# Pooled attention and a gated MLP on one core: keys tiled by head pair, leftovers in 32-column matmul tiles, keys turned by DMA

## Chip, cores and metric

One core of one Trainium2 chip. The metric is the device time of one execution in microseconds (us), the median of the runs. The kernel before took 309.03 us (308.74 to 309.35, 4 runs, the profiled one among them). The granted TensorE clock (the share of full speed that the throttle let through), averaged over the execution, is 0.997 to 1.000 in the kernel before.

Names: PE is TensorE, PEld its weight loads, DVE VectorE, ACT ScalarE, POOL GpSimd, SP SyncE, which issues most DMAs.

## The reference

```python
batch, n_heads, seq, head_dim = (8, 8, 576, 64)       # q, k, v; d_model 512, d_ff 2048
k_p = k.reshape(B, H, 72, 8, D).mean(axis=3)           # keys and values pooled by 8: 72 rows per head
v_p = v.reshape(B, H, 72, 8, D).mean(axis=3)
attn = softmax(q @ k_p.transpose / sqrt(D))            # per head: 576 x 72
x = (attn @ v_p).transpose(0, 2, 1, 3).reshape(B * S, H * D)   # 4608 tokens x 512
h = x @ w_in
return (h - np.tanh(h)) @ w_out                        # 4608 x 512, float32
```

## The kernel before

The MLP runs over nine groups of 512 tokens (0 to 8), each with an h phase (64 matmuls for `x @ w_in`, tanh and subtraction) and an o phase (64 matmuls for `@ w_out`). The attention of batch `nb` is woven into the o phase of group `nb - 1`, in rounds `u` of four o matmuls. Batch 0 is done alone at the start, and batch 1 lies in group 0's o phase.

A batch has 8 heads x 72 = 576 pooled key rows. Before, they lie in five tiles of 128 rows (the last half full) without regard to heads; a head pair's 144 rows cross tile borders, so three of the five score tiles need two accumulating matmuls:

```python
PAIRS = [[0], [0, 1], [1, 2], [2, 3], [3]]             # head pairs that a tile of keys touches
for n, hp in enumerate(PAIRS[t]):
    nc.tensor.matmul(dst, lhsT=KB[b % 2][:, hp * KBW + t * 128 : hp * KBW + (t + 1) * 128],
                     rhs=qTs[b][:, hp, c0:c1], start=(n == 0), stop=(n == len(PAIRS[t]) - 1))
```

KB holds the pooled keys, turned (head dimension on partitions) and padded with zeros. Before, PE turns the keys of batches 1 to 7 in the first round of the o phase, and DVE and ACT copy them to KB. The loads of the start:

```python
load_rows(k_rows, k_raw[0], 0, 0, 2)                   # SP: 512 KB of keys
load_q0(0, 4)                                          # ACT's queue: 512 KB of q
load_rows(k_rows, k_raw[0], 0, 4, 5)                   # SP: the 64 leftover rows, 128 KB
load_rows(k_rows, k_raw[0], 0, 2, 4)                   # SP: the other 512 KB of keys
load_q0(4, 8)                                          # ACT's queue: 512 KB of q
nc.scalar.dma_start(out=t0[:QT, :, R, :], in_=...)     # ACT's queue: the tail of q, 128 KB
# ... cut; later, batch 0's own order of work:
k_turn(0, 2); q_pe_transpose(0, (0, 1), "act")
pool_k(0, nc.vector, 4, 5); pool_k(0, nc.vector, 2, 4)
scores_wide(0, (0, 1)); warm_pe(5)                     # warm_pe: matmuls on zeros, to keep PE busy
k_turn(2, 5); q_pe_transpose(0, (2, 3), "act")
v_pe_pool(0, 3); scores_wide(0, (2,)); v_pe_pool(3, 5); scores_wide(0, (3, 4))
```

Batch 1's transposes of x, one round after the product that they turn:

```python
if u >= 9:
    if pend is not None:
        x_pe_transpose(1, *pend)
        pend = None
    if u <= 13:
        pend = (u - 9, av(1, u - 9, ps_any, False))
```

The softmax here doesn't subtract the row's maximum and nothing guards it: scores larger than these inputs give would overflow.

Of the kernel before, what the change touches and what calls it, by code (L numbers as in the profile page):

```python
# [27 lines left out]
NT = 5  # L28
D1 = D + 1
SCALE = 1.0 / (POOL * float(D) ** 0.5)  # L30
# [3 lines left out]
def kernel(  # L34
# [28 lines left out]
    v_rows = v.rearrange("b h (g j) d -> b (h g) (j d)", j=POOL)  # L63

# [4 lines left out]
    mask = const.tile([128, NT, 3, 1], FP32, name="mask")  # L69
    k_raw = [const.tile([128, NT, POOL * D], FP32, name=f"k_raw{i}") for i in range(2)]  # L70
    v_raw = [const.tile([128, NT, POOL * D], FP32, name=f"v_raw{i}") for i in range(2)]
    KBW = NT * 128
    STEP = KBW + 2 * G
    KB = [const.tile([128, NHP * KBW + 2 * G + KBW], BF16, name=f"KB{i}") for i in range(2)]
    q_bf = const.tile([128, R + 1, H, D], BF16, name="q_bf")
    warm = const.tile([128, 1], FP32, name="warm")
    VB = [const.tile([128, NT, 3, D1], BF16, name=f"VB{i}") for i in range(2)]
# [18 lines left out]
    def load_rows(src, dst, b, t0, t1):  # L96
        if t1 <= 4:
            return nc.sync.dma_start(
                out=dst[:, t0:t1, :],
                in_=src[b, t0 * 128 : t1 * 128, :].rearrange("(t p) n -> p t n", p=128),  # L100
            )
        return nc.sync.dma_start(out=dst[0:64, 4, :], in_=src[b, 512:576, :])

    def load_k(b, cuts=(0, 4, 5)):
        return [load_rows(k_rows, k_raw[b % 2], b, a, z) for a, z in zip(cuts, cuts[1:])]

    def load_v(b, cuts=(0, 4, 5)):
        return [load_rows(v_rows, v_raw[b % 2], b, a, z) for a, z in zip(cuts, cuts[1:])]
# [84 lines left out]
    def pool_v(b, eng, t0=0, t1=NT):  # L193
        r = v_raw[b % 2].rearrange("p t (j d) -> p t j d", d=D)[:, t0:t1, :, :]
        n = t1 - t0
        eng.tensor_tensor(  # L196
            out=r[:, :, 0:4, :], in0=r[:, :, 0:4, :], in1=r[:, :, 4:8, :], op=ALU.add
        )
        eng.tensor_tensor(  # L199
            out=r[:, :, 0:2, :], in0=r[:, :, 0:2, :], in1=r[:, :, 2:4, :], op=ALU.add  # L200
        )
        eng.tensor_tensor(
            out=r[:, :, 0, :], in0=r[:, :, 0, :], in1=r[:, :, 1, :], op=ALU.add
        )
        return eng.tensor_tensor(  # L205
            out=VB[b % 2][:, t0:t1, :, 0:D],
            in0=r[:, :, 0:1, :].to_broadcast([128, n, 3, D]),
            in1=mask[:, t0:t1, :, :].to_broadcast([128, n, 3, D]),
            op=ALU.mult,
        )  # L210

    def k_transpose(b, alloc):
        kd = kdups.pop(b)
        kb = KB[b % 2]
        for half in range(2):
            ps = alloc([128, 2, 2, G], FP32, "kT_ps")
            flat = ps.rearrange("p i a g -> p (i a g)")
            c = half * 4 * G
            while c < (half + 1) * 4 * G:
                t = c // 128  # L220
                n = min((t + 1) * 128, (half + 1) * 4 * G) - c
                nc.tensor.matmul(  # L222
                    flat[:, c - half * 4 * G : c - half * 4 * G + n],
                    lhsT=kd[:, t, :, :].rearrange("p a d -> p (a d)"),
                    rhs=ident[:, c - t * 128 : c - t * 128 + n],
                    start=True,
                    stop=True,
                )
                c += n
            step = KBW + 2 * G  # L230
            for par, eng in ((0, nc.vector.tensor_copy), (1, nc.scalar.copy)):
                off = 2 * half * step + par * G
                pr = slice(par * D, (par + 1) * D)
                eng(  # L234
                    out=kb[pr, off : off + 2 * step].rearrange("p (i x) -> p i x", x=step)[
                        :, :, 0:G
                    ],
                    in_=ps[pr, :, par, :],
                )

    E_tiles = {}
    PAIRS = [[0], [0, 1], [1, 2], [2, 3], [3]]

    def scores(b, t):
# [3 lines left out]
        qT = qTs[b]  # L248
        hs = S // 2
        for half in range(2):  # L250
            ps = ps_a.tile([128, hs], FP32, name="s_ps", tag="ps_a")
            for n, hp in enumerate(PAIRS[t]):
                nc.tensor.matmul(  # L253
                    ps[:, :],
                    lhsT=KB[b % 2][:, hp * KBW + t * 128 : hp * KBW + (t + 1) * 128],
                    rhs=qT[:, hp, half * hs : (half + 1) * hs],
                    start=(n == 0),
                    stop=(n == len(PAIRS[t]) - 1),
                )
            nc.scalar.activation(  # L260
                out=E[:, t, half * hs : (half + 1) * hs], in_=ps[:, :], func=ACT.Exp, scale=SCALE
            )

    XM = [
        [(0, 1, 3, 0), (1, 0, 3, 1), (2, 0, 1, 3)],
        [(2, 1, 3, 0), (3, 0, 3, 1), (4, 0, 1, 3)],
    ]
# [18 lines left out]
    def score_mms(b, t, dst, c0, c1):  # L286
        for n, hp in enumerate(PAIRS[t]):
            nc.tensor.matmul(  # L288
                dst,
                lhsT=KB[b % 2][:, hp * KBW + t * 128 : hp * KBW + (t + 1) * 128],  # L290
                rhs=qTs[b][:, hp, c0:c1],
                start=(n == 0),
                stop=(n == len(PAIRS[t]) - 1),
            )

    def av_half(b, blk, half, x_sb, alloc):
# [4 lines left out]
        for n, (t, s0, s1, h0) in enumerate(XM[half]):  # L301
            nc.tensor.matmul(  # L302
                ps[:, h0 : h0 + s1 - s0, :].rearrange("p h d -> p (h d)"),
                lhsT=E[:, t, c0 : c0 + 128],
                rhs=vb[:, t, s0:s1, :].rearrange("p h d -> p (h d)"),
# [179 lines left out]
    def load_q0(h0, h1):  # L485
# [5 lines left out]
    load_rows(k_rows, k_raw[0], 0, 0, 2)  # L491
    load_q0(0, 4)
    load_rows(k_rows, k_raw[0], 0, 4, 5)
    load_rows(k_rows, k_raw[0], 0, 2, 4)
# [3 lines left out]
    nc.vector.memset(zeros, 0.0)  # L498
# [3 lines left out]
    nc.vector.memset(k_raw[0][64:128, 4, :], 0.0)  # L502
# [3 lines left out]
    nc.gpsimd.memset(v_bf[64:128, 4, :], 0.0)  # L506
    nc.gpsimd.memset(q_bf[64:128, R, :, :], 0.0)
    nc.gpsimd.memset(mask[:, :, :, :], 1.0)
    mflat = mask.rearrange("p t s o -> p t (s o)")
    nc.gpsimd.affine_select(  # L510
        out=mflat,
        in_=mflat,
        compare_op=ALU.is_ge,
        fill=0.0,
        base=G,
        pattern=[[-16, NT], [-G, 3]],
        channel_multiplier=1,
    )
    nc.gpsimd.affine_select(
        out=mflat,  # L520
        in_=mflat,
        compare_op=ALU.is_ge,
        fill=0.0,
        base=-1,
        pattern=[[16, NT], [G, 3]],
        channel_multiplier=-1,
    )
    for i in range(2):
        nc.gpsimd.tensor_scalar_mul(VB[i][:, :, :, D:D1], mask[:, :, :, :], float(POOL))
    nc.gpsimd.dma_start(  # L530
        out=v_bf[:, 0:3, :], in_=v_rows[0, 0:384, :].rearrange("(t p) n -> p t n", p=128)
    )
    nc.gpsimd.dma_start(out=v_bf[:, 3, :], in_=v_rows[0, 384:512, :])
    nc.gpsimd.dma_start(out=v_bf[0:64, 4, :], in_=v_rows[0, 512:576, :])
# [3 lines left out]
    nc.gpsimd.memset(k_raw[1][64:128, 4, :], 0.0)  # L538
    nc.gpsimd.memset(v_raw[1][64:128, 4, :], 0.0)
    nc.gpsimd.memset(v_raw[0][64:128, 4, :], 0.0)  # L540
# [6 lines left out]
    def k_turn(ta, tb):  # L547
        kd = kdups[0]
        c0, c1 = ta * 128, min(tb * 128, 8 * G)
        ps = ps_any([128, 512], FP32, "kT_ps")  # L550
        for t in range(ta, tb):
            n = min(128, c1 - t * 128)
            nc.tensor.matmul(
                ps[:, t * 128 - c0 : t * 128 - c0 + n],
                lhsT=kd[:, t, :, :].rearrange("p a d -> p (a d)"),
                rhs=ident[:, 0:n],
                start=True,
                stop=True,
            )
        for par in range(2):  # L560
            pr = slice(par * D, (par + 1) * D)
            whole = [h for h in range(par, 8, 2) if h * G >= c0 and (h + 1) * G <= c1]
            h = whole[0]
            n = len(whole)
            o = (h // 2) * KBW + h * G
            p = h * G - c0
            nc.vector.tensor_copy(
                out=KB[0][pr, o : o + (n - 1) * STEP + G]
                if n == 1
                else KB[0][pr, o : o + n * STEP].rearrange("p (i x) -> p i x", x=STEP)[:, :, 0:G],  # L570
                in_=ps[pr, p : p + G]
                if n == 1
                else ps[pr, p : p + n * 2 * G].rearrange("p (i x) -> p i x", x=2 * G)[:, :, 0:G],
            )
        a, z = (3 * G, c1) if ta == 0 else (c0, 4 * G)
        o = KBW
        nc.vector.tensor_copy(out=KB[0][D:128, o + a : o + z], in_=ps[D:128, a - c0 : z - c0])
# [8 lines left out]
    def v_pe_pool(t0, t1):  # L586
        ps = ps_any([128, t1 - t0, D], FP32, "v_ps")
        for j in range(POOL):
            nc.tensor.matmul(
                ps[:, :, :],  # L590
                lhsT=ident[:, :],
                rhs=v_bf[:, t0:t1, j * D : (j + 1) * D],
# [176 lines left out]
```

## Time and profile before

| | before |
|---|---|
| median of the runs | 309.03 us |
| span of the profiled run | 307.3 us |
| PE busy | 97% |
| start of the h phase at full rate | 22.59 us |
| start of group 1 | 57.78 us |
| period of groups 1 to 6 | 31.74 us |

I cut the span in three stages: the start, until the h matmuls come without a break; the rest of group 0, which holds batch 1; and the six like periods with the end. The table of stretches has, behind each stretch, its length, then PE's busy time and count, those of PEld, DVE, ACT and POOL, the granted clock, the DMA share and GB/s. The kernel before:

```profile
0.00:22.59 22.59, 17.96 (x123) 9.34 (x124) 14.22 (x42) 10.47 (x21) 13.31 (x25) 1.00 1.06 223
22.59:57.78 35.19, 33.78 (x232) 17.49 (x232) 19.58 (x46) 19.21 (x37) 23.64 (x15) 1.00 1.08 275
57.78:307.30 249.52, 245.91 (x1353) 122.34 (x1351) 125.58 (x262) 118.82 (x232) 86.59 (x51) 1.00 0.53 136
```

The first stage has DMA busy throughout and PE idle for 4.6 us, 2.2 of them waiting for pooled keys. PE's timeline: start, length, line, operation, output<-inputs, shape, count, and in brackets the idle time before it with its releaser.

```profile
9.43 1.24 PE L479 MATMUL warm_ps<-xT 128*128 128x512 bf16 x5
12.11 0.31 PE L553 MATMUL kT_ps<-ident,kd 128*128 128x128 bf16 x3 [1.44 <-DVE kd L185]
```

PE waits 1.44 us for the pooled keys of the second piece.

### The profile page before, as it was taken

The page shows a single profiled execution, that of the slowest core. Times are in us where ns is not written, and L with a number is a line of the kernel's source. Part 1 is how long each engine was busy: PE and PEld are TensorE (multiplying, and loading weights), DVE is VectorE, ACT ScalarE, POOL GpSimd, SP SyncE. Part 2 cuts the span into 40 slices and gives each one's busy share as a digit, 9 for nine tenths or more (in the row PEclk, how much of TensorE's full clock was granted, in tenths as well). Part 3 has the DMA queues.
Part 4 walks back from the last instruction along what each step waited for, and adds up shares of the span by engine and source line. Part 5 has one row for each costly group of instructions (what it writes and reads, how often), then busy time and mean ns, then how long its engine had stood idle before and what let it go on. Part 6 is the DMA issues. An engine that isn't in the chain of part 4 may idle for free.

```text
span 307.3 us, 4716 instructions
## 1 busy us (share of the span) xinstructions
PE 297.7 (97%) x1707; PEld 149.2 (49%) x1707; DVE 159.4 (52%) x350; ACT 148.5 (48%) x289; POOL 123.5 (40%) x91
## 2 busy tenths in 40 slices
PE   7789999999999999999999999999999999999995
PEld 2454455445554455445544554455445544444443
DVE  5658714684348524861577066707472657207700
ACT  1657544466336642665166506651566246226511
POOL 8800996870694019801980079207920000000000
PEclk9999999999999999999999999999999999999999
DMA  7999999849654984498558954894521340011033
GB/s 231 229 213 305 251 188 332 253 102 325 187 108 105 300 230 112 97 271 241 105 111 211 319 113 120 209 293 116 112 60 37 80 99 2 34 68 34 3 65 72
DMA packets 61799, 48.74 MB, mean 159 GB/s; under 512 B 35536, under 2 KB 48656, under 8 KB 61776
## 3 DMA queue, kind: packets, MB, share of 16 engines
q1 hardware_dynamic: 55184, 42.35, 51.5%
q0 software_dynamic: 4848, 4.78, 9.5%
q10 hardware_dynamic: 1744, 1.31, 1.5%
q8 instruction: 13, 0.21, 0.3%
q14 instruction: 10, 0.08, 0.1%
HBM read 36.70 MB, written 9.44 MB: 150 GB/s over the span
## 4 chain that ended last, share of the span: by engine, by line
PE 82%; DMA 10%; POOL 3%; DVE 2%; issue 1%; SPq 0%; ACT 0%; POOLq 0%
PE o_ps L408 37%; PE hT_ps L380 36%; PE s_ps L253 4%; DMA w1b<-in_moe_w_in_dram 4%; PE x_ps L302 4%; DMA k_raw<-in_k_dram 3%; DMA w2b<-in_moe_w_out_dram 2%; DVE x_sb L312 1%; POOL k_raw L177 1%; DMA out_dram<-o_sb 1%; PE s_ps L288 1%; PE kT_ps L222 1%; POOL k_raw L180 0%; DVE rden L311 0%; PE xT_ps L342 0%
## 5 line engine op out<-in xcount | busy, mean ns | idle before, releaser
L408 PE MATMUL o_ps<-w2b,gT 128*128 128x512 bf16 x560 | 135.2, 379 | 0.1
L393 DVE TENSOR_TENSOR gT<-hT_ps,t_sb 128x512 bf16<-128x512 f32 x144 | 98.9, 691 | 59.1 <-ACT t_sb L391 58.3
L380 PE MATMUL hT_ps<-xT,w1b 128*128 128x512 bf16 x576 | 127.1, 379 | 0.9 <-ACT xT L349 0.5
L391 ACT ACTIVATE t_sb<-hT_ps 128x512 f32<-128x512 f32 x144 | 85.6, 597 | 39.2 <-PE hT_ps L380 38.7
L380 PEld LDWEIGHTS <-w1b 128*128 128x128 bf16 x576 | 55.9, 98 | 67.1 <-issue 1.4
L408 PEld LDWEIGHTS <-gT 128*128 128x128 bf16 x560 | 51.7, 98 | 49.6 <-issue 0.2
L417 ACT COPY o_sb<-o_ps 128x512 f32<-128x512 f32 x33 | 19.3, 586 | 75.6 <-PE o_ps L408 75.6
L128 POOL CAST q_bf<-q_raw 128x2048 bf16<-128x2048 f32 x7 | 13.2, 1892 | 79.0 <-DMA q_raw<-in_q_dram 77.9
L311 DVE RECIPROCAL rden<-x_ps 128x4 f32<-128x4 f32 x80 | 14.1, 176 | 59.1 <-PE x_ps L302 58.5
L312 DVE TENSOR_TENSOR x_sb<-x_ps,rden 128x256 bf16<-128x256 f32 x80 | 33.9, 424 | 2.8
L177 POOL TENSOR_TENSOR k_raw<-k_raw 128x1280 f32<-128x1280 f32 x7 | 20.2, 2888 | 18.3 <-DMA k_raw<-in_k_dram 18.3
L260 ACT ACTIVATE E<-s_ps 128x288 bf16<-128x288 f32 x60 | 21.4, 409 | 9.6 <-PE s_ps L253 9.6
L302 PE MATMUL x_ps<-VB,E 128*128 128x130 bf16 (+2 forms) x240 | 21.1, 221 | 0.0
L302 PEld LDWEIGHTS <-E 128*128 128x128 bf16 x240 | 17.1, 98 | 7.8
L196 POOL TENSOR_TENSOR v_raw<-v_raw 128x1280 f32<-128x1280 f32 x7 | 20.3, 2899 | 0.0
L253 PE MATMUL s_ps<-qT,KB 128*128 128x288 bf16 x96 | 16.7, 287 | 0.0
L253 PEld LDWEIGHTS <-KB 128*128 128x128 bf16 x96 | 9.2, 98 | 9.1 <-ACT KB L234 2.6
L205 POOL TENSOR_TENSOR VB<-v_raw,mask 128x960 bf16<-128x960 f32 x7 | 12.6, 1795 | 0.6
L199 POOL TENSOR_TENSOR v_raw<-v_raw 128x640 f32<-128x640 f32 x7 | 10.8, 1540 | 0.6
L180 POOL TENSOR_TENSOR k_raw<-k_raw 128x640 f32<-128x640 f32 x7 | 10.8, 1536 | 0.6
L185 POOL TENSOR_TENSOR kd<-k_raw 128x640 bf16<-128x640 f32 x7 | 10.8, 1539 | 0.5
L479 PE MATMUL warm_ps<-xT 128*128 128x512 bf16 x28 | 9.6, 466 | 1.3 <-DVE warm L500 1.3
(67 smaller groups left out, 107.0 us busy)
## 6 DMA issues: line engine op xcount, KB each, us to landing
k_raw<-in_k_dram SPq DMA_DIRECT2D x7, 1024.0 KB, 6.6
q_raw<-in_q_dram SPq DMA_DIRECT2D x7, 1024.0 KB, 12.7
v_raw<-in_v_dram SPq DMA_DIRECT2D x7, 1024.0 KB, 9.1
out_dram<-o_sb SPq DMA_DIRECT2D x38, 128.0 KB, 2.4
out_dram<-o_sb SPq DMA_DIRECT2D x16, 256.0 KB, 2.7
w1b<-in_moe_w_in_dram POOLq DMA_DIRECT2D x4, 512.0 KB, 12.8
w2b<-in_moe_w_out_dram POOLq DMA_DIRECT2D x4, 512.0 KB, 6.8
k_raw<-in_k_dram SPq DMA_DIRECT2D x2, 512.0 KB, 6.5
```

Of the source, the lines that this page charges most:

```text
L177: first = eng.tensor_tensor(out=r[:, :, 0:4, :], in0=r[:, :, 0:4, :], in1=r[:, :, 4:8, :], op=ALU.add)
L196: eng.tensor_tensor(out=r[:, :, 0:4, :], in0=r[:, :, 0:4, :], in1=r[:, :, 4:8, :], op=ALU.add)
L253: nc.tensor.matmul(ps[:, :], lhsT=KB[b % 2][:, hp * KBW + t * 128 : hp * KBW + (t + 1) * 128], rhs=qT[:, hp, half * hs : (half + 1) * hs], ...
L260: nc.scalar.activation(out=E[:, t, half * hs : (half + 1) * hs], in_=ps[:, :], func=ACT.Exp, scale=SCALE)
L302: nc.tensor.matmul(ps[:, h0 : h0 + s1 - s0, :].rearrange("p h d -> p (h d)"), lhsT=E[:, t, c0 : c0 + 128], rhs=vb[:, t, s0:s1, :].rearrang ...
L311: nc.vector.reciprocal(out=rden[:, :, :], in_=ps[:, :, D:D1])
L312: nc.vector.tensor_tensor(out=x_sb[:, half, :, :], in0=ps[:, :, 0:D], in1=rden[:, :, :].to_broadcast([128, 4, D]), op=ALU.mult,)
L380: nc.tensor.matmul(h_tiles[i][:, :], lhsT=w1b[:, fb, i * 128 : (i + 1) * 128], rhs=xT[:, fb, tok0 : tok0 + TG], start=(fb == 0), stop=(fb ...
L391: nc.scalar.activation(out=t_sb[:, :], in_=h_ps[:, :], func=ACT.Tanh)
L393: nc.vector.tensor_sub(out=gT[:, :], in0=h_ps[:, :], in1=t_sb[:, :])
L408: nc.tensor.matmul(o_ps[:, :], lhsT=gts[i][:, tb * 128 : (tb + 1) * 128], rhs=w2b[:, i, :], start=(i == 0), stop=(i == NHID - 1),)
L417: (nc.vector.tensor_copy if g == 0 and tb % 2 else nc.scalar.copy)(out=o_sb[:, :], in_=o_ps[:, :])
```

## The change

The intent: give each head pair its own 128-row tile (a pair has 144 rows), so that four of the five score tiles need one matmul, and collect the 16 rows left over per pair in a fifth tile at partitions 0, 32, 64 and 96. Its scores are four 32-column matmuls that can run side by side. Keys of batches 2 to 7 are turned by one DMA transpose per batch and placed into KB by GpSimd, which takes PE, DVE and ACT out of it. The core of the diff (cut):

```diff
+    def load_main(src, dst, b, t0, t1):
+        return nc.sync.dma_start(out=dst[:, t0:t1, :], in_=src[b, 0:128, t0:t1, :])
+    def load_left(src, dst, b):                        # four loads of 16 rows in place of one of 64
+        return [nc.sync.dma_start(out=dst[32 * t : 32 * t + LO, NM, :], in_=src[b, 128:PR, t, :])
+                for t in range(NM)]
...
+    def k_dma_transpose(b):
+        kT = work.tile([128, NT, 128], BF16, name="kT", tag="kT", bufs=1)
+        nc.sync.dma_start_transpose(out=kT[:, :, :], in_=kdups.pop(b)[...])
+    def k_place(b, eng):                               # three copies, on GpSimd
+        kb_main(KB[b % 2], kT[:, 0:NM, :], 0, NM, (eng, eng))
+        kb_left(KB[b % 2], kT[:, NM, :], eng)
+    def score_mms(b, t, dst, c0, c1):
+        for m in range(NM) if t == NM else (t,):
+            o = m * KP + (128 if t == NM else 0)
+            w = 32 if t == NM else 128
+            p = 32 * m if t == NM else 0
+            nc.tensor.matmul(dst[p : p + w], lhsT=KB[b % 2][:, o : o + w],
+                             rhs=qTs[b][:, m, c0:c1], start=True, stop=True)
... the start
-    load_rows(k_rows, k_raw[0], 0, 0, 2)
+    load_main(k_pairs, k_raw[0], 0, 0, 2)
     load_q0(0, 4)
-    load_rows(k_rows, k_raw[0], 0, 4, 5)
-    load_rows(k_rows, k_raw[0], 0, 2, 4)
+    load_left(k_pairs, k_raw[0], 0)
+    load_main(k_pairs, k_raw[0], 0, 2, 4)
     load_q0(4, 8)
... batch 0
-    k_turn(2, 5)
+    k_turn_left()
+    k_turn(2, 4)
     q_pe_transpose(0, (2, 3), "act")
-    v_pe_pool(0, 3)
-    scores_wide(0, (2,))
-    v_pe_pool(3, 5)
-    scores_wide(0, (3, 4))
+    v_pe_pool()
+    scores_wide(0, (2, 3, 4))
... batch 1: transposes of x two rounds later instead of one
-            if pend is not None:
-                x_pe_transpose(1, *pend)
+            if u >= 11 and pend:
+                x_pe_transpose(1, *pend.pop(0))
... batches 2 to 7
-                if i == 3:
+                if i == (3 if g == 1 else 8):
+                    k_dma_transpose(nb)
+                    k_place(nb, nc.gpsimd.tensor_copy)
...
-                    if u == 0:
-                        k_transpose(nb, ps_b1)
```

The values are laid out in the same way (three masked matmuls of 130 columns in place of 195, 130 and 65). Two things are not in the cut. The memset that clears the leftover tile now stands ahead of the loads, so the first leftover load waits for DVE and goes out at 1.77 us (before: 1.33). And in batches 2 to 7 the exponentials follow the matmuls of both halves, so that the narrow matmuls of both stand together.

## The prediction

> **What bounds the kernel now.** I read the page's totals first, to see which engine could be the bound, and then the table of stretches, to see whether it is the bound in every stage.
>
> ```profile
> PE 297.7 (97%) x1707; PEld 149.2 (49%) x1707; DVE 159.4 (52%) x350; ACT 148.5 (48%) x289; POOL 123.5 (40%) x91
> ```
>
> ```profile
> 30.00:40.00 10.00, 9.69 (x63) 4.71 (x60) 6.45 (x14) 5.26 (x11) 9.88 (x8) 1.00 1.09 252
> ...
> 121.43:135.25 13.82, 13.82 (x66) 6.23 (x64) 9.88 (x15) 9.54 (x16) 8.01 (x5) 1.00 0.55 145
> 135.25:153.17 17.92, 17.92 (x117) 9.80 (x116) 7.19 (x24) 6.31 (x16) 8.24 (x5) 1.00 0.78 198
> 248.40:276.02 27.62, 27.62 (x129) 12.54 (x128) 11.07 (x16) 11.90 (x20) 0.00 (x0) 1.00 0.15 47
> ```
>
> The second and third number of each row are the stretch's length and PE's busy time. From 58 us on they are equal, at granted clock 1.00, so only fewer or shorter matmuls can shorten the steady part. The chain of work repeats with starts at 57.95, 89.69, 121.43 and so on to 248.40: six periods of 31.74 us, each an h phase (13.81) and an o phase with the next batch's attention (17.92). The last group, without attention, has 13.81 for each phase. So one batch's attention costs 31.74 - 27.62 = 4.12 us of PE. From the same rows, 64 matmuls of 512 columns take 13.81 us, 215.8 ns each, which is 2.4 columns per ns and 2.5 ns more. A matmul of N columns in the stream then costs N/2.4 + 2.5 ns (an estimate from this trace). I use it in place of the durations in the groups, which overlap.
>
> What is in the 4.12 us I read from PE's timeline in group 2.
>
> ```profile
> 103.34 1.03 PE L408 MATMUL o_ps<-w2b,gT 128*128 128x512 bf16 x4
> 104.20 0.43 PE L222 MATMUL kT_ps<-ident,kd 128*128 128x128 bf16 x6
> 104.47 1.02 PE L408 MATMUL o_ps<-w2b,gT 128*128 128x512 bf16 x4
> 105.43 0.42 PE L253 MATMUL s_ps<-qT,KB 128*128 128x288 bf16 x2
> 105.69 1.03 PE L408 MATMUL o_ps<-w2b,gT 128*128 128x512 bf16 x4
> 106.55 0.65 PE L253 MATMUL s_ps<-qT,KB 128*128 128x288 bf16 x4
> 107.04 1.03 PE L408 MATMUL o_ps<-w2b,gT 128*128 128x512 bf16 x4
> ```
>
> Starts tell the cost. The six key transposes hold PE 0.27 us (104.20 to 104.47). A pair of score matmuls accumulated in both halves (x4) takes 0.49 us, a single one (x2) 0.245. Between 104.47 and 105.43 there are only four matmuls (0.86 us), so 0.10 us is idle: the waits name it as "PEld L253 <- ACT KB L234", 0.4 us on the weight loader, six times.
>
> Batch 1 is different: its attention lies in group 0's o phase:
>
> ```profile
> 48.61 1.02 PE L408 MATMUL o_ps<-w2b,gT 128*128 128x512 bf16 x4
> 49.48 0.69 PE L342 MATMUL xT_ps<-ident,x_sb 128*128 128x128 bf16 x4
> 50.00 0.52 PE L302 MATMUL x_ps<-VB,E 128*128 128x130 bf16 x6
> 50.36 1.03 PE L408 MATMUL o_ps<-w2b,gT 128*128 128x512 bf16 x4
> ```
>
> One such round takes 50.36 - 48.61 = 1.75 us, yet its matmuls need 0.86 + 0.22 + 0.34 = 1.43. The missing 0.32 us is the transpose waiting for x_sb from DVE, which has one o chunk (0.86) in which to do two reciprocals and two products (2 x 0.176 + 2 x 0.424 = 1.2 us).
>
> **What the Trainium skill says.** "TensorEngine Tiling (Array Packing)", Key Properties: tiles of the array work independently, and "Changing tiling mode (not just tile) drains the TensorE". "TensorE: Matmul & The Clock Gate", Part 3, Measured speedup vs the span model, gives about 4 ns per further tile and a measured 2.38x for three column tiles. Its section Single matmul latency has (398 + N)/2.4 ns, so 166 ns of fill and drain that a stream hides. The trace has 379 ns for 512 columns and 287 for 288, as that formula gives, but those ends are modelled. Nothing in this trace has 32-column tiles: all rows read 128*128, so neither the drain nor the concurrency can be checked before. "DMA: Bandwidth & Descriptors", Rules for kernel authors, warns that transfers under 64 KB are mostly overhead; the leftover loads become 32 KB each. Here an issue costs SP 0.5 to 0.6 us whatever its size.
>
> **The change, part by part.**
> *Scores (batches 2 to 7).* Before, eight matmuls per half: 16 x 122.5 = 1.96 us. After, four full ones per half, 8 x 122.5 = 0.98, and twice four 32-column ones. If those four run together, each set takes about 120 + 3 x 4 = 132 ns, 0.27 in all. The halves are issued together, so there is one switch into 32-column mode and one out; at one fill and drain each, 2 x 0.17 = 0.33. Sum 1.58, a gain of 0.38 us per batch.
> *Key transposes.* Six matmuls leave PE, 0.27, and the 0.10 us wait for KB goes too, if GpSimd is in time: 0.37. DVE and ACT lose two copies each, which gains nothing as neither bounds.
> *Weighted values.* 195 + 130 + 65 = 390 columns become 3 x 130: no change.
> Steady sum: 0.75 x 6 = 4.5 us gained.
> *Batch 1.* The transpose of x lags two rounds in place of one, so the 0.32 us stall of five rounds goes: 1.6 us gained. Wide scores: three fewer 512-column matmuls (0.65) less one switch pair (0.33); the tail of 64 columns saves almost nothing and pays a pair. Together about zero.
> *Batch 0.* The tail pays a switch pair in a PE-bound stretch: 0.25 lost. The start is a chain of latencies: key load, pooling, turning, scores, exponentials, x. The second key piece is now issued behind four leftovers instead of one (3 x 0.6 us on SP), all value tiles are pooled before the last three score tiles, and the first half of x now needs the leftover tile, the last exponential. I put 1.0 us lost there, with 0.2 us of it hidden where the w2b load makes PE wait at 40.5. GpSimd has to issue two more value loads before w1b (about 1.5 us), but the 16 DMA engines are busy to nine tenths then, and the same bytes go through: nothing.
> Sum: -4.5 - 1.6 + 0.25 + 0.8 = -5.0, and 0.3 us for the first of the rivals below: -4.7, from 309.0 to 304.3 us.
>
> **The rivals.**
> *GpSimd and SP become the wait.* Keys now go pooling, DMA transpose, three placements behind the pooling of values, before the first score.
>
> ```profile
> 113.86 1.89 POOL L128 CAST q_bf<-q_raw 128x2048 bf16<-128x2048 f32 x1 [18.19 <-DMA q_raw<-in_q_dram]
> 115.69 0.61 POOL L131 CAST q_bf<-q_raw 64x512 bf16<-64x512 f32 x1
> 116.27 2.89 POOL L177 TENSOR_TENSOR k_raw<-k_raw 128x1280 f32<-128x1280 f32 x1
> ```
>
> GpSimd waits 18 us for q here, so it has room. Keys are pooled by 122.4, values 7.1 us later, placements take about 0.9 (288 + 224 + 64 columns at the cast's 0.92 ns, and three starts), so 130.4; the first score of that group is near 137. SP pays one transpose (about 1.5 us by the 1.25 of those that turn four blocks) and six more issues (3.5), which delays q by up to 5 us: still in time. Only batch 2 is tight: its q cast starts at 58.05, SP's five transposes end at 66.5, the key transpose lands (2.4 us, as its like) near 70.5, placing ends at 71.5, the first score is due near 72.6. One stall of up to 1.5 us, 0.3 expected. If it recurred in every group, 6 x 1 us, the time would be about 309.
> *The 32-column tiles run one after another.* Then 8 x 0.12 us instead of 0.27: 0.7 us per batch, which eats the gain; about 308.5. For it: no such tile in the trace, and weight loads that share rows. Against: the page's measured 2.38x.
> *The switch costs almost nothing*, or is hidden by loading ahead: 0.3 us more per batch, about 302.
> *The start is bound by the loads anyway*: 0.8 us back, 303.5.
>
> **Range and chances.** The steady gain is a count of matmuls and rests on one unknown, the tiles; I give concurrency 85%. The drain gives +-1.5 us, the start +-1. So 304.3 us, 301.9 to 307.2 in 8 of 10. 2% faster is 302.8: it needs cheap switches and an undelayed start, 0.2. Slower by 2% (315.2) needs a recurring stall and serial tiles, 0.02.
>
> **What would show it.** In the changed profile the chain's period should be near 31.0 us, PE should still fill it, rounds of group 0's o phase should be near 1.43 us, and the 32-column matmuls of one half should start within some 20 ns of each other with about 0.6 us for the two halves and both switches. Wrong would be: PE idle before the first score with POOL as releaser, starts 120 ns apart, or a first group that begins over 2 us later than now.

## The result, and the profile after

307.71 us (307.39 to 307.94, 4 runs) against 309.03: ratio 0.9956, 95% interval 0.9939 to 0.9974. A ratio here is the mean time of one kernel's fast runs over the mean of the other's fast runs of the same rounds, so not quite the ratio of the medians quoted. The change is a small gain, under the 2% that would count as faster, and the time lies above the predicted range, 301.9 to 307.2. The totals and the row of the granted clock (40 slices, tenths of full speed) of the changed kernel:

```profile
PE 292.6 (96%) x1662; PEld 143.2 (47%) x1662; DVE 155.1 (51%) x333; ACT 145.2 (47%) x276; POOL 126.9 (42%) x120
...
PEclk9879999999999999999999999999999999999999
```

PE has 5.1 us less to do, but the span fell by 1.6 us only. The clock row was 9 throughout before; now slices two and three read 8 and 7. The three stages, changed kernel:

```profile
0.00:28.33 28.33, 19.61 (x116) 9.61 (x116) 12.56 (x37) 10.26 (x21) 12.12 (x29) 0.88 1.08 235
28.33:61.72 33.39, 32.73 (x232) 17.14 (x231) 19.73 (x47) 18.65 (x35) 25.75 (x18) 1.00 0.96 244
61.72:305.70 243.98, 240.29 (x1318) 116.42 (x1315) 122.77 (x250) 116.25 (x221) 89.07 (x74) 1.00 0.59 143
```

| stage | before | after | difference | predicted |
|---|---|---|---|---|
| start | 22.59 | 28.33 | +5.74 | +0.8 |
| rest of group 0 | 35.19 | 33.39 | -1.80 | -1.35 |
| the periods and the end | 249.52 | 243.98 | -5.54 | -4.2 (with 0.3 for batch 2) |
| span | 307.30 | 305.70 | -1.60 | -4.7 |

So the expected gain is there, and larger than I said; 5.7 us of it is given back in the first 28 us. PE's timeline of group 2's o phase, changed kernel, answers to the lines of 103 to 107 us in the prediction:

```profile
106.34 1.89 PE L440 MATMUL o_ps<-w2b,gT 128*128 128x512 bf16 x8
108.06 0.41 PE L282 MATMUL s_ps<-qT,KB 128*128 128x288 bf16 x2
...
111.64 1.03 PE L440 MATMUL o_ps<-w2b,gT 128*128 128x512 bf16 x4
112.59 0.43 PE L282 MATMUL s_ps<-qT,KB 128*32 128x288 bf16 x8
112.95 1.25 PE L440 MATMUL o_ps<-w2b,gT 128*128 128x512 bf16 x5
```

The o phase begins with two unbroken rounds (x8): no key transposes, no wait for KB. The eight 32-column matmuls (128*32) begin 0.09 us after the o stream ends (111.64 + 0.863 = 112.50), and the next o matmul starts 0.36 us later. Eight one after another would need 8 x 0.1225 = 0.98 us, so they ran side by side. The single records of the trace, which the merged line hides, show it directly: the four of one half start at 112.592, 112.595, 112.598 and 112.602, the next four from 112.724, one set of four 132 ns after the other. That is the 132 ns that the prediction had from the Trainium skill's 4 ns per further tile. To the third digit the switch in took 0.093 us, from the end of the o stream to the first set; the switch out took 0.097 us, from the end of the second set's 132 ns to the next o matmul. Together with both switches the two halves cost 0.45 us, where I had put 0.60. The period is 30.81 us (starts at 61.72, 92.53, 123.33, ...).

A round of group 0's o phase was 1.75 us; in the changed kernel PE's timeline has 1.45 from one start to the next:

```profile
55.19 1.03 PE L440 MATMUL o_ps<-w2b,gT 128*128 128x512 bf16 x4
...
56.64 1.03 PE L440 MATMUL o_ps<-w2b,gT 128*128 128x512 bf16 x4
```

Now the start of the changed kernel. First PE's timeline, then the chain of waits (start, length, what), then SP's queue:

```profile
11.03 0.23 PE L243 MATMUL kT_ps<-ident,kd 128*128 128x128 bf16 x1 [0.59 <-DVE kd L194]
16.21 0.39 PE L243 MATMUL kT_ps<-ident,kd 128*128 128x128 bf16 x2 [4.95 <-DVE kd L194]
...
17.25 2.34 PE L596 MATMUL v_ps<-v_raw,ident 128*128 128x320 bf16 x8
```

```profile
0.81 5.31 DMA q_raw<-in_q_dram
6.14 8.38 DMA k_raw<-in_k_dram
```

```profile
0.81 0.46 SPq L101 DMA_DIRECT2D k_raw<-in_k_dram  x1
1.77 2.26 SPq L105 DMA_DIRECT2D k_raw<-in_k_dram  x4
6.14 13.46 SPq L101 DMA_DIRECT2D k_raw<-in_k_dram  x2
```

PE waits 4.95 us for the second piece of keys (1.44 before), and afterwards runs slowly: eight matmuls of 320 columns take 2.1 us, 266 ns each, about 1.2 columns per ns in place of 2.4. The chain says what came first: a load of q, and only when it lands, at 6.12, does the load of keys begin. In SP's queue the four leftovers are issued by 4.03, and then SP does nothing for 2.1 us before the main piece goes out at 6.14 (before, it went out at 1.95). SP waits, but SP has no data to wait for: this load writes a buffer that nobody has used. The trace's list of waits on SP's queue puts the 2.1 us down to the load of q (`SPq L101 <- DMA q_raw`). The list of waits in the compiled program has the answer. SP's first rows, changed kernel:

```
1 DMACopy k_raw<-in_k_dram 128x2x512
2 DMACopy k_raw<-in_k_dram 16x512 [waits DVE]
3 DMACopy k_raw<-in_k_dram 16x512 x3
4 DMACopy k_raw<-in_k_dram 128x2x512 [waits DMAHW0]
```

(The wait for DVE is the memset named above.) In this program every load from SP or ACT signals its landing on one of eight semaphores, DMAHW0 to DMAHW7, which are used in turn, in the order of the program and over both queues. The kernel before had six such loads at the start (three of keys, three of q); four leftovers in place of one make nine. The ninth reuses semaphore 0, and so it must wait until semaphore 0's load, the first half of q, has landed. The ninth in the program's own order is the main key piece, on which everything hangs. (Five kernels of the runs below show the same: where nine loads are in flight the ninth waits for DMAHW0, in e6_before_four the second main piece and in e1_main_first the fourth leftover; in e5_before_three, e8_no_ninth and e9_tail_late, with eight, no load of keys at the start has such a wait.)

That is the theory. The rivals are these: the small loads are slow in themselves, or the key piece is late because it is issued behind them; or batch 0's new order of work is what costs.

### The profile page after: what moved, and what is told of

It reads as the page before. It is cut to its first block, busy times and chain, and to the rows that moved or that the text cites. A ratio compares the mean times of both kernels' runs of the same rounds, so it can differ in the third digit from the quotient of the medians.

```text
span 305.7 us, 4698 instructions
## 1 busy us (share of the span) xinstructions
PE 292.6 (96%) x1662; PEld 143.2 (47%) x1662; DVE 155.1 (51%) x333; ACT 145.2 (47%) x276; POOL 126.9 (42%) x120
## 4 chain that ended last, share of the span: by engine, by line
PE 89%; DMA 5%; DVE 2%; ACT 1%; issue 0%; SPq 0%
PE o_ps L440 40%; PE hT_ps L412 39%; PE x_ps L330 4%; PE s_ps L282 3%; DMA k_raw<-in_k_dram 3%; DMA q_raw<-in_q_dram 2%; DVE gT L425 1%; PE xT_ps L374 1%; DMA out_dram<-o_sb 1%; PE v_ps L596 1%; PE qT_ps L159 1%; ACT E L312 1%; DVE x_sb L344 0%; ACT t_sb L423 0%; ACT xT L381 0%
## 5 line engine op out<-in xcount | busy, mean ns | idle before, releaser
L440 PEld LDWEIGHTS <-gT 128*128 128x128 bf16 x560 | 52.5, 98 | 52.0 <-issue 1.4
L330 PE MATMUL x_ps<-VB,E 128*128 128x130 bf16 x240 | 20.9, 220 | 0.5 <-ACT E L312 0.5
L282 PE MATMUL s_ps<-qT,KB 128*128 128x288 bf16 (+5 forms) x128 | 16.8, 290 | 0.1
L282 PEld LDWEIGHTS <-KB 128*128 128x128 bf16 (+1 forms) x128 | 7.1, 96 | 10.4 <-issue 3.8
L381 ACT CAST xT<-xT_ps 128x256 bf16<-128x256 f32 (+1 forms) x14 | 6.1, 434 | 7.7 <-PE xT_ps L374 7.5
```

The costliest lines, as they stand in the source:

```text
L282: nc.tensor.matmul(dst[p : p + w], lhsT=KB[b % 2][:, o : o + w], rhs=qTs[b][:, m, c0:c1], start=True, stop=True,)
L330: nc.tensor.matmul(ps[:, 2 * n : 2 * n + 2, :].rearrange("p h d -> p (h d)") if n < 2 else ps.rearrange("p (a s) d -> p a s d", s=2)[:, :, ...
L440: nc.tensor.matmul(o_ps[:, :], lhsT=gts[i][:, tb * 128 : (tb + 1) * 128], rhs=w2b[:, i, :], start=(i == 0), stop=(i == NHID - 1),)
```

## The experiments

Twelve kernels; all gave correct results. "Full h" is the time from which the h matmuls come in one stream in the profiled run, but for one wait of 0.35 us that all have (22.59 before, 28.33 after). Each ratio is to the kernel before. The changed kernel has no run in these calls; where I set a run against its 307.71 us, the kernel before ran within 0.2 us of its 309.03 in that call.

| run | built on | time us | ratio to before (95%) | full h us |
|---|---|---|---|---|
| e1_main_first | after | 306.20 | 0.9899 (0.9870 to 0.9927) | 26.99 |
| e5_before_three | before | 308.78 | 0.9997 (0.9982 to 1.0012) | 22.45 |
| e6_before_four | before | 313.93 | 1.0163 (1.0135 to 1.0192) | 28.18 |
| e7_warm | after | 306.10 | 0.9908 (0.9891 to 0.9924) | 26.98 |
| e8_no_ninth | after | 303.11 | 0.9806 (0.9790 to 0.9822) | 23.12 |
| e2_lag_alone | before | 307.51 | 0.9954 (0.9939 to 0.9969) | 22.27 |
| e3_pe_turn | after | 311.33 | 1.0077 (1.0062 to 1.0092) | 28.10 |
| e4_wide_left | after | 311.61 | 1.0080 (1.0061 to 1.0099) | 29.45 |
| e9_tail_late | after | 303.91 | 0.9840 (0.9826 to 0.9854) | 23.26 |
| e10_less_warm | after | 303.55 | 0.9823 (0.9810 to 0.9835) | 24.51 |
| e12_v_late | after | 303.91 | 0.9841 (0.9818 to 0.9864) | 23.34 |
| e11_v_early | after | 303.29 | 0.9829 (0.9805 to 0.9854) | 23.05 |

### Three or four small loads in the kernel before

The cleanest test leaves the changed kernel alone. In the kernel before, only the 64-row load of batch 0's leftover keys is cut:

```diff
-    load_rows(k_rows, k_raw[0], 0, 4, 5)
+    for r0, r1 in zip((0, 32, 48), (32, 48, 64)):      # the other run: 0, 16, 32, 48, 64
+        nc.sync.dma_start(out=k_raw[0][r0:r1, 4, :], in_=k_rows[0, 512 + r0 : 512 + r1, :])
```

> The kernel before, with only the 64-row key load of batch 0 cut into three (32, 16 and 16 rows): eight loads in flight at the start, two small pieces more to issue ahead of the main piece. Theory (reuse of eight completion semaphores): no load waits, 309.0 us within 0.7. Rival (small pieces are slow in themselves, or the later issue behind them is the cost): 310.5 to 312.

> The kernel before, with that load cut into four of 16 rows: nine loads in flight. Theory: the second main key piece waits for the first q piece to land (near 6 us), the keys land 4 us later, PE idles and cools, and the time is 313 to 314.5 us. Rival (size or issue time of the small pieces): a third more than the loss of the run with three pieces, so at most 0.2 to 1 us above it.

SP's queue, three pieces:

```profile
1.31 1.46 SPq L494 DMA_DIRECT2D k_raw<-in_k_dram  x3
2.81 16.14 SPq L98 DMA_DIRECT2D k_raw<-in_k_dram  x2
```

SP's queue, four pieces:

```profile
1.32 2.09 SPq L494 DMA_DIRECT2D k_raw<-in_k_dram  x4
6.28 12.76 SPq L98 DMA_DIRECT2D k_raw<-in_k_dram  x2
```

PE's timeline, four pieces:

```profile
16.06 0.45 PE L556 MATMUL kT_ps<-ident,kd 128*128 128x128 bf16 x3 [5.54 <-DVE kd L185]
```

With eight loads in flight the next one follows at once (2.81) and the time is that of before, 308.78 us. With nine it goes out at 6.28, PE idles 5.5 us, the clock row reads 8 and 7 in the same slices as after the change, and the time is 313.93 us. Small pieces cost nothing (the warning about loads under 64 KB, which the prediction cites, did not show here); the ninth load costs 5.15 us. The rival on size and issue falls.

### The changed kernel with one load sent later

```diff
     load_q0(4, 8)
-    nc.scalar.dma_start(out=t0[:QT, :, R, :], in_=q[0, :, QA:S, :]...)
...
     scores_wide(0, (0, 1))
+    nc.scalar.dma_start(out=t0[:QT, :, R, :], in_=q[0, :, QA:S, :]...)
```

> The changed kernel with only the 128 KB tail of q sent later (after the first exponentials), so that eight loads are in flight at the start; the leftovers stay ahead of the second main key piece. Theory: no load waits, that piece goes out near 4.1 us instead of 6.1 and lands near 10.5 to 11.5 instead of 14.5; the time is 303.3 to 304.8 us. Rival (the order of the pieces, leftovers ahead, is the cost rather than the semaphore): 306.5 or more.

The leftovers still stand ahead of the main piece, and nothing of the work is reordered; only the number of loads in flight falls to eight. SP's queue in this run (the line holds this load and the next batch's):

```profile
3.69 15.43 SPq L101 DMA_DIRECT2D k_raw<-in_k_dram  x2
```

303.91 us, 3.8 less than the changed kernel, with the clock row at 9 throughout. Full h at 23.26 in place of 28.33: 5.07 of the 5.74 us lost at the start. The 0.67 us that are left go to batch 0's new order of work, the 0.80 us for which PE waits for values in this run among it; I had put 0.8 there. (In this run 0.5 us comes back as a wait at the start of group 2, told below.)

### Swapping the order only

```diff
+    load_main(k_pairs, k_raw[0], 0, 2, 4)
     load_left(k_pairs, k_raw[0], 0)
-    load_main(k_pairs, k_raw[0], 0, 2, 4)
```

> The changed kernel with one pair of lines swapped: the second main piece of batch 0's keys is loaded ahead of the four leftover pieces. Theory (the ninth load in flight must wait for a completion semaphore that an earlier load still holds): the main piece goes out near 1.5 us instead of 6.1 and lands near 10.4, the wait falls on the last small piece, PE's first h matmuls start near 24 us instead of 28.3, and the time is 303.5 us (302.5 to 304.5). Rival (the first batch's new order of work costs the 5.7 us: all values pooled before the last three score tiles, leftover tile needed for the first half of x): time stays within 1 us of 307.7.

306.20 us: a miss. The wait moved as expected, to the fourth leftover piece, and that did not help much. DVE's timeline shows why:

```profile
12.14 0.42 DVE L186 TENSOR_TENSOR k_raw<-k_raw 128x256 f32<-128x256 f32 x1 [4.28 <-DMA k_raw<-in_k_dram]
...
13.14 0.68 DVE L186 TENSOR_TENSOR k_raw<-k_raw 128x512 f32<-128x512 f32 x1
```

DVE pools the leftover tile (128x256) ahead of the main one (128x512), in program order, and the last piece landed at 12.1. I had seen only which load waits, not who stands in line behind it. PE's matmuls after the gap were slow here too. One of the four runs took 304.47 us, the others 306.1 to 306.4. I have no trace of that one, but its granted clock is 1.000, the others' 0.987 to 0.994. So its clock did not fall after the gap, which fits the cost of the cold clock measured next.

### The cold clock alone

```diff
     k_turn_left()
+    warm_pe(22)
     k_turn(2, 4)
```

> The changed kernel with 22 more idle-filling matmuls (4.7 us of PE at full clock) put in the gap in which PE waits for the second key piece. The wait stays; if 1.2 to 1.7 us of the 5.7 us lost at the start come from matmuls at a lowered clock after the gap (value pooling took 2.3 us there instead of about 1.1), the time is 306.2 us (305.8 to 306.6). If the clock costs nothing, 307.7.

306.10 us, as expected. PE's timeline of this run:

```profile
16.42 0.28 PE L243 MATMUL kT_ps<-ident,kd 128*128 128x128 bf16 x2 [0.38 <-DVE kd L194]
...
16.99 1.25 PE L596 MATMUL v_ps<-v_raw,ident 128*128 128x320 bf16 x8
```

The keys are as late as in the changed kernel (16.42 against 16.21), but value pooling takes 1.1 us from start to start in place of 2.1, and full h comes at 26.98, 1.35 us earlier. If the three parts simply add, the start's 5.74 us are about 0.7 of new order, 1.35 of cold clock, and the remaining 3.7 of the late keys themselves.

### The parts of the steady gain

The longer lag alone, in the kernel before (the `pend` lines of the diff, nothing else):

> The kernel before with only the longer lag of batch 1's transposes of x (two rounds instead of one). Theory: five waits of 0.32 us go from a stretch that PE bounds: 307.4 us (307.0 to 307.8). Rival (the stretch is bound by the w2b loads or the next h phase waits for x anyway): 309.0 within 0.3.

307.51 us, within the range, and 1.33 us below the kernel before of the same call (308.84). In the trace group 1 starts at 56.18 us in place of 57.78, but 0.32 us of that is a start that happened to be earlier (full h 22.27 against 22.59): the stretch in between is 1.28 us shorter. The step holds, at 1.3 us; of the five waits four were 0.3 us long, and the fifth, of a half-filled block, about 0.2.

The keys of batches 2 to 7 turned by PE again, in the changed kernel:

```diff
-                    k_dma_transpose(nb)
-                    k_place(nb, nc.gpsimd.tensor_copy)
...
+                    if u == 0:
+                        k_transpose(nb, ps_b1)
```

> The changed kernel, but the keys of batches 2 to 7 are turned by TensorE again (five 128-column matmuls and copies by DVE and ACT in the first round of the o phase), no DMA transpose and no GpSimd placing. Theory: 0.28 us of matmuls and about 0.1 us of waiting for KB come back per batch, the period is 31.2 us instead of 30.8, 6 x 0.38 = 2.3 us: 310.0 us (309.5 to 310.5). Rival (the DMA transposes and six further issues per batch on SP cost something elsewhere that this gives back): 307.7 or less.

311.33 us, 3.6 above the changed kernel where I expected 2.3; the period is 31.40 us, 0.59 above. PE's timeline:

```profile
107.57 0.44 PE L243 MATMUL kT_ps<-ident,kd 128*128 128x128 bf16 x5
107.85 1.03 PE L440 MATMUL o_ps<-w2b,gT 128*128 128x512 bf16 x4
109.01 0.42 PE L282 MATMUL s_ps<-qT,KB 128*128 128x288 bf16 x2
```

The transposes take 0.28 us as I said. The wait for KB is 109.01 - 107.85 - 0.86 = 0.30 us, not 0.10: in the new layout the first score needs the copy of a whole half, 288 columns (0.44 us on DVE), and then ACT's copy, which began only when DVE's had ended. So the DMA path is worth 0.59 us per batch in this layout, more than the 0.37 it is worth against the kernel before. Nothing on SP or GpSimd takes it back.

The leftover scores with full-width weights (a second buffer KL, 128 columns per pair with only that pair's 16 filled):

```diff
-            w = 32 if t == NM else 128
-            p = 32 * m if t == NM else 0
-            nc.tensor.matmul(dst[p : p + w], lhsT=KB[b % 2][:, o : o + w], ..., start=True, stop=True)
+            nc.tensor.matmul(dst, lhsT=(KL if left else KB)[b % 2][:, o : o + 128], ...,
+                             start=(not left or m == 0), stop=(not left or m == NM - 1))
```

> The changed kernel with the leftover scores done by four accumulating 128-column matmuls (weights padded with zeros) in place of four 32-column ones. Theory (32-column ones run together: 0.45 us for both halves with both switches): 8 x 0.1225 = 0.98 us instead, 0.53 us per batch, 3.2 us for six batches and about 0.4 for the first two: period 31.35, 311.3 us (310.8 to 311.8). If the narrow ones ran one after another, or the switches ate the gain: 307.7 within 0.5.

311.61 us, 3.9 above the changed kernel; the period is 31.32, so 0.51 per batch. The start was 1.1 us longer as well, which I did not take apart. The narrow tiles pay for themselves, with the switches, by about what I said (0.98 less 0.45). Both this run and the one before it carry the ninth load, like the changed kernel, so they compare with 307.71 us.

### A start without the waiting load

Main piece first, the tail of q later, main keys pooled and turned ahead of the leftovers, `warm_pe(10)` in place of 5:

```diff
+    load_main(k_pairs, k_raw[0], 0, 2, 4)
     load_left(k_pairs, k_raw[0], 0)
-    load_main(k_pairs, k_raw[0], 0, 2, 4)
...
-    pool_k(0, nc.vector, 4, 5)
     pool_k(0, nc.vector, 2, 4)
+    pool_k(0, nc.vector, 4, 5)
...
+    nc.scalar.dma_start(out=t0[:QT, :, R, :], ...)     # the tail of q
-    warm_pe(5)
-    k_turn_left()
+    warm_pe(10)
     k_turn(2, 4)
+    k_turn_left()
```

> The changed kernel with a start in which no load waits for another: the main key piece ahead of the leftovers, the 128 KB tail of q sent only after the first exponentials (so eight loads are in flight, not nine), the main keys pooled and turned ahead of the leftover tile, and ten filling matmuls instead of five. Theory (the wait for a load's semaphore and the cold clock after it are the lost 5.7 us less about 1): main keys land near 10.4 us, no clock drop, the h phase is full from about 23.5 us instead of 28.3, 302.9 us (302.2 to 303.7). If the new order of the first batch's work costs more than I say, 304 to 306.

303.11 us, 5.7 below the kernel before of the same call (308.84) and the best of all. With five filling matmuls:

> The start without a waiting load, with five filling matmuls as in the changed kernel, not ten. If the ten were needed to keep the clock up, value pooling shows about 2.3 us again and the time is 304 to 304.5 us; if the short gap that is left (about 1.1 us) does no harm, 303.1 us within 0.4.

303.55 us. In the profiled run value pooling took 2.3 us again and full h came at 24.51. But the granted clock was 0.994 and 0.993 in two of the four runs and 1.000 in the other two (302.90 and 303.59 us): with five the clock falls in some executions, with ten it fell in none of four (0.998 to 1.000). The median was only 0.4 us longer for that reason, and because the run above loses 0.9 us later which the trace of this one does not. PE's timeline of the run with ten, at the start of group 2:

```profile
88.21 1.02 PE L412 MATMUL hT_ps<-xT,w1b 128*128 128x512 bf16 x4 [0.73 <-DMA xT<-x_sb]
```

PE comes early enough here to meet the tight spot that I had seen for batch 2. There it hardly shows in the keys but in x: SP issues the twelve loads of batch 3 in a row (69.7 to 77.2 us), then outputs, and only from 80.9 the transposes of x. Two tries to loosen it:

```diff
 # both: in group 1 only, batch 3's values after the fourth transpose of x
-                        load_v(nb + 1)
+                        if g > 1: load_v(nb + 1)
...
+                    if u == 11 and g == 1: load_v(nb + 1)
 # the second: batch 0's value loads ahead of GpSimd's mask work
```

> The start without a waiting load, and in group 1 only the five value loads of batch 3 go to SP's queue after the fourth transpose of x instead of ahead of all of them. In the run with the repaired start PE waited 0.7 us at the start of group 2 for a transpose of x which SP had issued late behind these loads, and period 1 was 31.7 us instead of 30.8. Theory: that wait goes, 302.2 us (301.8 to 302.7). If the value pooling of batch 3 becomes late instead: 303 or more.

> As the run before it, and batch 0's value loads are issued ahead of GpSimd's mask work (about 2.3 us earlier), since PE waited 1.1 us for values at 13.1 us. If values are the end of the start's chain: 301.5 us, 0.7 below the run before it. If the loads only share the same bandwidth, so that keys and q come later by what values gain: no difference (within 0.4).

Both miss. With the values later, the wait at group 2 is gone (period 30.81), but batch 3's values now land at 95.6 us, and group 3 starts 1.2 us late. About half of that is a wait for keys, which GpSimd places behind the late pooling of the values, the other half a wait for x of the same kind as before. PE's timeline of this run:

```profile
103.67 0.42 PE L282 MATMUL s_ps<-qT,KB 128*128 128x288 bf16 x2 [0.40 <-POOL KB L234]
...
119.54 1.67 PE L412 MATMUL hT_ps<-xT,w1b 128*128 128x512 bf16 x7 [0.43 <-DMA xT<-x_sb]
```

The time is 303.91 us, runs from 302.7 to 305.6. With the early values added PE no longer waits for values at the start; the chain there now runs through the second half of q instead, and full h comes only 0.3 us earlier. The median is 303.29 us, runs from 302.6 to 305.5. Within this spread neither differs from 303.11, and why it is wider than before is open (the clock is 0.998 or more in all of them). In the first of the two the wait is moved along, not removed; the kept trace of the second, its fastest run, has 0.2 us of it.

## Why the prediction was wrong

**The start: the failed step.** The prediction says that the second key piece "is now issued behind four leftovers instead of one (3 x 0.6 us on SP)", and puts 1.0 us lost on the start, 0.8 net. It cost 5.74 us. I counted the new loads as issue time. What they did is bring the loads in flight from six to nine, one more than there are semaphores for them, and the ninth, which waits 2.1 us for an unrelated load, heads the chain of the start. Cutting one load in the kernel before into four, and sending one load later in the changed kernel, show it from both sides (+5.15 and -3.8 us). The 0.67 us that remain without that wait are close to the 0.8 that I had sized. The issue time that I did count (3 x 0.6 us) did not show: two more pieces without a ninth load left the time at 308.78 us.

The test I named for the start ("a first group that begins over 2 us later than now") is the one that struck: group 1 begins 3.9 us later. I had also dismissed GpSimd's additional value loads; in the changed kernel its fourth w1b load waited 3.22 us for a value load, by the same rule with another set of eight. No run tests whether that costs anything, but with it left as it is the start is within 0.5 to 0.7 us of before.

**The steady part: right, and undersized.** 0.93 us per batch in place of 0.75. The transposes and the wait for KB gave the 0.37 us expected. The term that was off is the pair of switches: 0.33 us estimated, 0.19 measured (0.093 in, 0.097 out); the two sets side by side took the 0.26 to 0.27 us expected. The rival of serial tiles is refuted, the rival of cheap switches is half right.

**Batch 1: the mechanism right, the size partly luck.** The lag alone is worth 1.3 us where I had 1.6. The stage gained 1.80 in place of 1.35 all the same, because the rest of it, which I had put at 0.25 lost, gained 0.5. No run takes that rest apart; three pairs of switches at 0.19 us in place of 0.33 would make 0.4 of the difference (an estimate from the numbers above).

**GpSimd and SP as the wait: right for this kernel.** In group 2 GpSimd waits for the key transpose and is still in time; the timeline of POOL, changed kernel:

```profile
105.50 0.42 POOL L233 COPY KB<-kT 64x288 bf16<-64x288 bf16 x1 [4.50 <-DMA kT<-kd]
...
106.29 0.24 POOL L237 COPY KB<-kT 64x64 bf16<-64x64 bf16 x1
```

Keys are placed by 106.53 and needed at 108.06, 1.5 us to spare where I had reckoned with over six: SP issues without a break from 94.94 to 104.02 us, and the key transpose goes out last of that row. The first group's 0.3 us did not show in the changed kernel, I take it because its late start gave SP time; 0.5 to 0.9 us showed, as a wait for x, in two runs whose start was repaired.

**The sums.** One step of the prediction's arithmetic is told too briefly: the split of 215.8 ns into 2.4 columns per ns and 2.5 ns does not follow from one length. Its score lines give the second length (four matmuls of 288 columns in 0.49 us, 122.5 ns each), and with both the split comes out. With the start as I sized it the prediction's sum would have given 309.0 + 0.8 - 1.8 - 5.5 = 302.5 us; the repaired start measures 303.1 with its 0.9 us in group 1.

## What to carry to other kernels

Count the loads that are in flight at once, not only their bytes and issue times: cutting one load into four can make an unrelated, critical load wait for a landing, and moving one uncritical load out of that window gave back 3.8 us here. When an issuing queue sits idle ahead of a load into an unused buffer, look in the compiled program at what its instruction waits on. And when a chain gets shorter, look at once for the next tight queue: the repaired start met SP's order of issues one group later.

## What the Trainium skill lacked or had wrong

- Semaphores of loads: "DMA: Bandwidth & Descriptors" says to dedicate a semaphore to a DMA (Rules for kernel authors) and not to let two in flight share one. No page that I read says what this costs a program that has fewer semaphores than loads in flight: here the next load was not issued until an earlier one had landed. Eight are used in turn for SP and ACT: eight loads in flight, 308.78 us; nine, 313.93 us.
- Tiling modes: "TensorEngine Tiling (Array Packing)", Key Properties, gives no cost for the drain of a switch. Here the switch in cost 0.093 us and the switch out 0.097, which is less than the fill and drain of 166 ns each that I had borrowed from a formula.
- Clock: "TensorE: Matmul & The Clock Gate", Part 1, gives half rate after an idle window of about 3.4 us that is free-running. The changed kernel agrees (4.95 us idle, then 266 ns for 320 columns). With two gaps of 0.67 and 1.49 us, between which PE ran nine short matmuls, the clock fell as well in the trace (2.3 us for the same pooling) and, by the granted clock, in two of the four runs of that kernel; gaps of 1.21 and 0.80 us in another run left it up. The page helps to expect it, not to decide it.
